# Scratch stores of the first block sent after its last word, and words placed by a model in which TensorE waits for them

## The chip, the cores and the metric

One core of one Trainium2 chip runs the kernel. The time is the device time of the whole program in microseconds; of three runs of the kernel before the median is 587.93 us (587.58 to 592.4). The engines are named as in the profile: PE is the matrix engine (TensorE, with PEld its weight loads), DVE the vector engine, ACT the scalar engine, POOL is GpSimd, and SP is the queue from which nearly all DMAs are issued.

## The reference

Three stages follow one another on 1536 tokens of width 512: attention with four sink tokens and a window of 128, a dense layer with a leaky rectifier, and a layer of eight experts with a capacity.

```python
attn_out = _attn_ref(q, k, v, n_sink=4, window=128)      # 2 x 8 heads x 768 x 64
x = attn_out.transpose(0, 2, 1, 3).reshape(1536, 512)
h = x @ w_in                                             # w_in  512 x 2048, float64
x = (np.maximum(0.01 * h, h) @ w_out).astype(float32)    # w_out 2048 x 512, float64
...                                                      # x then goes through the experts: each token to one of 8
```

The two weights of the dense layer are 64-bit floats in memory. The kernel turns them into 32-bit floats itself.

## The kernel before, in words

The tokens go through the dense layer in six blocks of 256. Attention for the tokens of the next block is cut into small steps, which are put between the matmuls of the current block. The first block (`block0`, L2080) is special, because the weights are still being loaded and converted while it runs.

**Weights.** `w_in` and `w_out` are each cut into 16 chunks, f = 0 to 15, x = 0 for `w_in` and x = 1 for `w_out`. `FFN.seq` gives the order, numbered n: (0,0), (0,1), then (1,0) to (15,0) as n = 2 to 16, then (1,1) to (15,1) as n = 17 to 31. `FFN.load` (L978) puts the 512 KB of a chunk into one of five raw buffers (`RAW = 5`). `FFN.convert` (L1002) makes three DVE instructions of a chunk, called words here: low word (L1014), sign (L1018), tail (L1024). From n = 4 on the chunks are converted in pairs (4,5), (6,7), ...: low, low, sign, sign, tail, tail. When a chunk's words have been emitted, the load of chunk n + 5 is emitted on SP; it needs the raw buffer that the tail of chunk n releases.

**Split.** For products in fp32r a converted chunk is split in two parts, wh on ACT (L1042) and wl on POOL (L1043). `w_in` chunks from f = 5 on are split before their first use, `w_out` chunks from f = 10 on as well (`AHEAD = (5, 10)`); the others are used whole in block 0 and split later. SBUF doesn't hold all the parts, so those of f = 0, 1, 14 and 15 are also stored to a scratch in HBM (L1047) and read back two blocks later (L1068). In `split` each store is emitted right after its part.

**Order of block 0.** PE first makes `hps` for f = 0 to 15 (L1090, `ffn.first`), and then adds up `y` for f = 0 to 13 (L1138, `ffn.second`); f = 14 and 15 are done in block 1. Between them lie 21 attention steps, five units' worth: per unit of a tile and a group of heads the turn (L561) and its low part on DVE (L583, L587), the scores (L614) with a masked copy and a maximum on DVE (L624, L629), the exponentials on ACT (L637), the norm (L645, L646 on DVE, L648 on POOL), the transpose (L672, copied by ACT at L684 and masked by POOL at L687), the product with v (L710) and its low part on DVE (L729, `pv_low`). The scores take four PSUM buffers in a ring of four, and the last of these is the one that `pv_low` of the unit before reads.

**What sets the order.** Every engine runs its instructions in the order in which the program emits them, SP its DMAs too: a DMA that has to wait holds back all that stand behind it. On DVE the words are placed among the attention work by a small planner, `Pace` (L63). It keeps two clocks, `pe` and `dve`. Each piece of PE work adds its cost to `pe` (L69), a word adds `WORD_US = 0.6` to `dve`, and an attention step on DVE sets `dve` to the later of both clocks plus its cost, after `fill` has placed words while `dve < pe + SLACK` (`SLACK = 1.5`). `need` (L2001) places words at once where a chunk is about to be used. PE's clock does not wait for words in the kernel before.

Of the kernel before, what the change touches and what calls it, by code (L numbers as in the profile page):

```python
# [8 lines left out]
F32 = mybir.dt.float32  # L9
# [35 lines left out]
SLACK = 1.5  # L45
AHEAD = (5, 10)
WORD_US = 0.6
ROUTE = (2, 4, 6, 9, 10, 11, 14)
HOLD, TAIL = 4, 1
QUIET = 2  # L50
# [2 lines left out]


class Call:
    def __init__(self, f, us):
        self.f, self.us = f, us

    def __call__(self):
        self.f()  # L60
# [2 lines left out]
class Pace:  # L63


    def __init__(self):
        self.pe = self.dve = 0.0
        self.fill = lambda: None

    def tensor(self, us):  # L70
        self.pe += us

    def vector(self, us, wait=0.0):
        self.fill()
# [873 lines left out]
class FFN:  # L948
# [12 lines left out]
    def __init__(self, nc, pools, A, xt, cap):  # L961
        self.nc, self.p, self.A = nc, pools, A
        self.xt, self.CAP = xt, cap
        self.DM, self.DFF = A["shape_in"]
        self.K = self.DM // P
        self.NF = self.DFF // P
        self.wide = A["w_wide"]
        self.w, self.v, self.raw, self.g, self.y = {}, {}, {}, {}, {}
        self.ahead, self.x0 = AHEAD, []
        self.seq = [(0, 0), (0, 1)] + [(f, x) for x in range(2) for f in range(1, self.NF)]  # L970
        self.phase, self.late = 0, {}
        n = max(0, self.NF - self.CAP)
        self.saved = set(range(n)) | set(range(self.NF - n, self.NF))
        self.scr = self.p["dram"].tile([self.NF, 4, P, 512], F32, name="wscr") if n else None
# [23 lines left out]
    def convert(self, n, bank):  # L998


        nc, c = self.nc, self.p["c"]
        if n >= len(self.seq):  # L1002
            return []
        f, x = self.seq[n]
        at = {}

        def low_word():
            at["w"] = self.raw[f, x].rearrange("p (n two) -> p n two", two=2)
            if bank:
                pool, tag = self.bank(n % 2)  # L1010
                at["u"] = self.p[pool].tile([P, 512], I32, tag=tag, name="word")
            else:
                at["u"] = at["v"] = c.tile([P, 512], I32, tag="c", name="cvt")
            nc.vector.tensor_scalar(at["u"], at["w"][:, :, 1], 3, 0x3FFFFFF8, op0=ALU.logical_shift_left,  # L1014
                                    op1=ALU.bitwise_and)

        def sign():
            nc.vector.scalar_tensor_tensor(at["u"], at["w"][:, :, 1], -0x40000000, at["u"], op0=ALU.bitwise_and,  # L1018
                                           op1=ALU.bitwise_or)

        def tail():
            if bank:
                at["v"] = c.tile([P, 512], I32, tag="c", name="cvt")
            nc.vector.scalar_tensor_tensor(at["v"], at["w"][:, :, 0], 29, at["u"], op0=ALU.logical_shift_right,  # L1024
                                           op1=ALU.bitwise_or)

        def take():
            r = self.raw.pop((f, x))
            if not self.wide:
                at["v"] = c.tile([P, 512], F32, tag="c", name="cvt")  # L1030
                nc.vector.tensor_copy(at["v"], r)
            self.v.setdefault(f, {})[x] = at["v"].bitcast(F32)

        return [Call(g, WORD_US) for g in (low_word, sign, tail) if self.wide] + [Call(take, 0 if self.wide else WORD_US)]

    def split(self, f, x, eng):

        nc, c = self.nc, self.p["c"]
        t = self.v[f].pop(x)
        h = c.tile([P, 512], F32R, tag="c", name="wh")  # L1040
        l = c.tile([P, 512], F32R, tag="c", name="wl")
        nc.scalar.copy(h, t)  # L1042
        eng.tensor_tensor(out=l, in0=t, in1=h.bitcast(F32), op=ALU.subtract)  # L1043
        self.w.setdefault(f, {})[x] = (h, l)
        if f in self.saved:
            for a, t in enumerate((h, l)):
                nc.sync.dma_start(out=self.scr[f, 2 * x + a], in_=t.bitcast(F32))  # L1047

    def split_x0(self):

# [812 lines left out]
def build(tc, A, n_sink, window, capacity):  # L1863
    nc = tc.nc
# [13 lines left out]
    with ExitStack() as es:  # L1878
# [32 lines left out]
        pace = Pace()  # L1911
# [15 lines left out]
        if ring:  # L1927
# [3 lines left out]
            ffn = FFN(nc, p, A, xt, FFN.CAP)  # L1931
# [13 lines left out]
        if not ring:  # L1945
            pool(rawst, "raw", bufs=nraw, side="right")
            ffn = FFN(nc, p, A, xt, FFN.CAP - FEWER // 4)
# [18 lines left out]
        def some(calls, n):  # L1966
            for f in calls[:n]:
                f()
            del calls[:n]
# [12 lines left out]
        def word():  # L1982

            if not conv:
                if chunk >= len(ffn.seq):
                    return False
                conv.extend(convert())
            f = conv.pop(0)
            f()
            pace.dve += f.us  # L1990
            return True

        def fill():

            while started and pace.dve < pace.pe + SLACK and word():
                pass
# [3 lines left out]
        def need(f, x):  # L2000

            while x not in ffn.v.get(f, ()) and x not in ffn.w.get(f, ()):
                word()
# [13 lines left out]

        rate = max(1, -(-rt.NU * rt.E // ROUTE[4]))
        ex = Experts(nc, tc, p, A, rt, ident)
# [18 lines left out]
        def second():  # L2038
            j, f, i = pending.pop(0)
            if j == 0:  # L2040
                need(f, 1)
                pace.tensor(1.4 if ffn.in_parts(0, f, 1) else 1.88)
            if j == 1:
                split(0, f, 1)
            last = i == ffn.NF - 1
            if j == late and i >= ffn.NF - HOLD:

                ffn.second(j, f, i == 0, last, range(TPB - 1))
                held.append((j, f, i))
                if last:  # L2050
                    for t in range(TPB - 1):
                        rt.evac(j * TPB + t, ffn.y[j][t])
                return
            ffn.second(j, f, i == 0, last, range(TPB))
            del ffn.g[j, f]
            if j == 0:
                splits.extend([(f, 1)] * (not ffn.in_parts(0, f, 1)))
            elif i < n_ev or j == late:
                del ffn.w[f]
            if j > 1 and i < n_ev:  # L2060
                ffn.reload(ffn.order(j)[ffn.CAP + i])
            if last:
                ts = tuple(range(j * TPB, (j + 1) * TPB))
                for t, y in zip(ts, ffn.y.pop(j)):
                    rt.evac(t, y)
                routing.extend(route(ts, True))
                if j == late - 2 and rt.NU:
                    routing.insert(-1, ex.rank)
# [11 lines left out]
        def block0():  # L2080

            NF, last_t, ndone = ffn.NF, 2 * TPB - 1, 0
            pace.pe, pace.dve = 0.0, 1.7
            count = next((n + 1 for n, x in enumerate(steps) if x[0] == last_t), len(steps))
            for s in range(2 * NF - LAG):
                x, f = divmod(s, NF)
                if x == 0:
                    need(f, 0)
                    ffn.first(0, f)
                    pace.tensor(1.42 if ffn.in_parts(0, f, 0) else 1.95)  # L2090
                    if not ffn.in_parts(0, f, 0):
                        splits.append((f, 0))
                    ffn.leak(0, f)
                    if f == 0 and ffn.ahead[0] < NF:
                        ffn.split_x0()
                    fill()
                    for a in range(f + 2 if f else 0, f + 3):
                        if ffn.ahead[0] <= a < NF:
                            need(a, 0)
                            ffn.split(a, 0, nc.gpsimd)  # L2100
                    if f == NF - 1:
                        while conv:
                            word()
                        ffn.phase = 1
                        for a in range(LAG):
                            ready(a)
                else:
                    pending.append((0, f, f))
                    second()
                    fill()  # L2110
                    if f + LAG < NF - 1:
                        ready(f + LAG)
                    if splits and not splits[0][1]:
                        split(1)
                while ndone < min(count, max(1, count * (s + 1) // (2 * NF - LAG - 1))):
                    step()
                    ndone += 1
                fill()
            while word():
                pass  # L2120
            pending.extend((0, f, f) for f in range(NF - LAG, NF))
            ffn.phase = 2

        started = 1
# [6 lines left out]
        for j in range(1, NB):  # L2131
# [9 lines left out]
            for i, f in enumerate(ffn.order(j)):  # L2141
# [20 lines left out]
                some(clears, rate)  # L2162
                if routing and i in ROUTE:
                    routing.pop(0)()
# [86 lines left out]
```

## Time and profile before

| | |
|---|---|
| median of 3 runs | 587.93 us (587.58 to 592.4) |
| the profiled execution, its own time | 592.37 us |
| its span | 590.6 us |
| mean granted clock of TensorE | 0.975 |
| PE busy / PEld / DVE / ACT / POOL | 561.6 / 482.3 / 342.4 / 292.0 / 186.1 us |
| DVE words of the pairs, L1014 + L1018 + L1024 | 28 chunks of 3 |
| scratch stores L1047 | 16 of 256 KB |

PE is busy for 95% of the span, but this is an average: block 0 ends at 105.4 us, and in it DVE is the fuller engine. The stretches are best read one by one, with the granted clock beside the busy times, since a busy PE at a lower clock gives less. The profiled execution lies 4.4 us above the median.

### The profile page before, as it was taken

How to read it: one execution, taken by the hardware profiler on the slowest of the kernel's cores; microseconds unless marked ns; L12 is line 12 of the kernel's file. 1: busy time of each engine (PE TensorE's matmuls, PEld its weight loads, DVE VectorE, ACT ScalarE, POOL GpSimd, SP SyncE). 2: the span in 40 equal slices, each digit the busy share in tenths (PEclk: the TensorE clock that was granted, in tenths of full speed). 3: DMA queues.
4: the chain of work that ended last, by engine and by line, in shares of the span. 5: the costliest groups of instructions: out<-in, count | busy, mean ns of one | idle time of the engine just before them, and what ended most of it. 6: DMA issues, size and time to landing. Idle time of an engine off the chain costs nothing.

```text
span 590.6 us, 11359 instructions
## 1 busy us (share of the span) xinstructions
PE 561.6 (95%) x3801; PEld 482.3 (82%) x3801; DVE 342.4 (58%) x823; ACT 292.0 (49%) x859; POOL 186.1 (32%) x330
## 2 busy tenths in 40 slices
PE   8988979999999999999999999999799989999993
PEld 7777636888888888888888888878699888988782
DVE  6997878667434544444435422765467656636992
ACT  6766635766444445444444333552345434425771
POOL 5665667722432243224222331231102000001110
PEclk9998989999999999999999999999699979999998
DMA  8885794699333023302320257560557645444940
GB/s 232 239 261 163 268 296 133 216 278 346 91 108 90 19 72 90 109 19 63 89 72 2 83 162 248 172 191 28 188 177 232 224 150 191 144 157 140 329 145 7
DMA packets 83577, 91.85 MB, mean 156 GB/s; under 512 B 42979, under 2 KB 51171, under 8 KB 83488
## 3 DMA queue, kind: packets, MB, share of 16 engines
q1 hardware_dynamic: 81504, 85.68, 47.6%
q0 software_dynamic: 1984, 5.13, 2.4%
q8 instruction: 38, 0.62, 0.5%
q14 instruction: 51, 0.42, 0.2%
HBM read 72.01 MB, written 20.09 MB: 156 GB/s over the span
## 4 chain that ended last, share of the span: by engine, by line
PE 71%; issue 8%; DVE 7%; DMA 7%; POOL 3%; ACT 2%; another core or an unknown queue 0%; POOLq 0%; SPq 0%; DVEq 0%; ACTq 0%
PE hps L1090 20%; PE y L1138 19%; PE ph L1585 11%; PE py L1634 8%; PE ops L710 3%; PE sps L614 2%; DMA out<-ys,gt 2%; DVE word L1018 2%; DVE word L1014 1%; POOL wl L1043 1%; DMA places<-x,rsi 1%; DMA craw<-in_moe_w 1%; DVE cvt L1024 1%; PE pps L672 1%; DMA rawo<-in_moe_w_out 1%
## 5 line engine op out<-in xcount | busy, mean ns | idle before, releaser
L1138 PE MATMUL y<-wh,gp 128*128 128x512 f32 x344 | 126.8, 409 | 1.2 <-ACT gp L1118 0.7
L1120 POOL TENSOR_TENSOR gp<-g,gp 128x256 fp32r<-128x256 f32 x77 | 57.1, 742 | 181.8 <-ACT gp L1118 167.7
L1109 DVE TENSOR_TENSOR g<-hps,g 128x256 f32<-128x256 f32 x80 | 33.7, 422 | 104.2 <-ACT g L1108 103.8
L1090 PE MATMUL hps<-xth,wh 128*128 128x256 f32 x320 | 92.0, 288 | 0.4 <-DVE g L1109 0.4
L1090 PE MATMUL hps<-xth,wl 128*128 128x256 f32 x320 | 90.6, 283 | 0.0
L1090 PE MATMUL hps<-xtl,wh 128*128 128x256 f32 x320 | 90.5, 283 | 0.0
L1449 DVE TENSOR_TENSOR cw<-craw,cw 128x512 fp32r<-128x512 f32 x128 | 83.3, 695 | 8.6 <-ACT cw L1447 6.8
L1138 PEld LDWEIGHTS y<-wh,gp 128*128 128x128 f32 x344 | 64.4, 188 | 16.2 <-ACT gp L1118 1.5
L1447 ACT CAST cw<-craw 128x512 fp32r<-128x512 f32 x112 | 63.4, 620 | 23.7 <-PE py L1634 23.1
L1108 ACT ACTIVATE g<-hps 128x256 f32<-128x256 f32 x80 | 30.6, 382 | 85.2 <-PE hps L1090 84.8
L1138 PE MATMUL y<-wl,gp 128*128 128x512 f32 x172 | 67.6, 393 | 0.6 <-POOL wl L1043 0.6
L1585 PE MATMUL ph<-xt,cw 128*128 128x256 f32 (+2 forms) x444 | 64.6, 312 | 0.0
L1634 PE MATMUL py<-cw,ht 128*128 128x512 f32 x264 | 63.9, 398 | 0.3 <-DVE ht L1622 0.3
L1090 PEld LDWEIGHTS hps<-xth,wh 128*128 128x128 f32 x320 | 60.4, 189 | 4.4 <-DVE g L1109 1.3
L1585 PEld LDWEIGHTS ph<-xt,cw 128*128 128x128 f32 x444 | 63.6, 212 | 0.1
L1090 PEld LDWEIGHTS hps<-xtl,wh 128*128 128x128 f32 x320 | 60.3, 188 | 2.2
L1090 PEld LDWEIGHTS hps<-xth,wl 128*128 128x128 f32 x320 | 60.2, 188 | 0.0
L1634 PEld LDWEIGHTS py<-cw,ht 128*128 128x128 f32 x264 | 49.0, 188 | 11.6 <-DVE ht L1622 0.7
L1643 POOL DMA_INDIRECT out<-ys,gt x11 | 11.3, 1032 | 120.1 <-DVE ys L1642 114.5
L1118 ACT CAST gp<-g 128x256 fp32r<-128x256 f32 x80 | 32.9, 411 | 21.7 <-DVE g L1109 21.7
L1138 PEld LDWEIGHTS y<-wl,gp 128*128 128x128 f32 x172 | 32.5, 189 | 5.3 <-POOL wl L1043 1.2
L637 ACT ACTIVATE pm<-pm,mx 128x132 f32<-128x132 f32 (+1 forms) x80 | 31.8, 401 | 10.1 <-DVE mx L629 10.1
(247 smaller groups left out, 996.6 us busy)
## 6 DMA issues: line engine op xcount, KB each, us to landing
craw<-in_moe_w SPq DMA_DIRECT2D x128, 256.0 KB, 3.4
rawi<-in_moe_w_in SPq DMA_DIRECT2D x16, 512.0 KB, 4.8
rawo<-in_moe_w_out SPq DMA_DIRECT2D x16, 512.0 KB, 5.9
places<-zero SPq DMA_DIRECT2D x24, 257.0 KB, 5.8
wh<-wscr SPq DMA_DIRECT2D x16, 256.0 KB, 2.9
wl<-wscr SPq DMA_DIRECT2D x16, 256.0 KB, 2.8
xg<-places SPq DMA_DIRECT2D x12, 257.0 KB, 4.3
natv<-in_v SPq DMA_DIRECT2D x12, 256.0 KB, 4.3
```

What stands on the lines that cost most here:

```text
L637: self.nc.scalar.activation(a, a, AF.Exp, bias=mx[:, pr, e:e + 1], accum_out=su[:, pr, e, 0:1])
L710: nc.tensor.matmul(ps[64 * e:64 * e + 64, pr, :], lhsT=l, rhs=r, start=(x == 0 and not (late and pr)), stop=(x == len(mm[0]) - 1 and not l ...
L1090: nc.tensor.matmul(ps, lhsT=w, rhs=x, start=(n == 0), stop=(n == len(mm) - 1))
L1108: nc.scalar.activation(g, ps, AF.Copy, scale=0.01)
L1109: nc.vector.tensor_tensor(out=g, in0=ps, in1=g, op=ALU.max)
L1118: nc.scalar.copy(gp[:, 0], g)
L1120: eng.tensor_tensor(out=gp[:, 1], in0=g, in1=gp[:, 0].bitcast(F32), op=ALU.subtract)
L1138: nc.tensor.matmul(y, lhsT=l, rhs=r, start=(start and n == 0), stop=(stop and n == len(mm) - 1))
L1447: nc.scalar.copy(h, t)
L1449: eng.tensor_tensor(out=l, in0=t, in1=h.bitcast(F32), op=ALU.subtract)
L1585: nc.tensor.matmul(self.ph[f][:, sl], lhsT=self.w[e, "a", h, k][w][:, f * P:(f + 1) * P], rhs=self.xt[:, a, k, sl], start=(m == 0), stop=( ...
L1634: nc.tensor.matmul(self.py[n], lhsT=x, rhs=w, start=(h == 0 and f == 0 and m == 0), stop=(h == self.NH - 1 and f == self.HF - 1 and m == 2))
```

## The change

Two edits. Stores: `split` no longer issues its stores but puts them in a list, and `FFN.store` issues the whole list after block 0's last word; from then on (`phase > 1`) each split stores at once, as before. Planner: when the last word of a chunk is placed, the `dve` clock is noted under the chunk's key; a PE product that uses this chunk then starts, in the model, no earlier than that time, and `PARTS_US = 2.0` later if it uses the two parts.

```diff
+PARTS_US = 2.0
...
-    def tensor(self, us):
-        self.pe += us
+        self.ready = {}
+
+    def tensor(self, us, key=None, wait=0.0):
+        self.pe = max(self.pe, self.ready.get(key, -1.0) + wait) + us
...
-        return [Call(g, WORD_US) for g in (low_word, sign, tail) if self.wide] + [Call(take, 0 if self.wide else WORD_US)]
+        return [Call(g, WORD_US) for g in (low_word, sign, tail) if self.wide] + [Call(take, 0 if self.wide else WORD_US, (f, x))]
...
         if f in self.saved:
-            for a, t in enumerate((h, l)):
-                nc.sync.dma_start(out=self.scr[f, 2 * x + a], in_=t.bitcast(F32))
+            self.stores += [(f, 2 * x + a, t) for a, t in enumerate((h, l))]
+            if self.phase > 1:
+                self.store()
+
+    def store(self):
+        while self.stores:
+            f, n, t = self.stores.pop(0)
+            self.nc.sync.dma_start(out=self.scr[f, n], in_=t.bitcast(F32))
...
             pace.dve += f.us
+            if f.key:
+                pace.ready[f.key] = pace.dve
...
-                pace.tensor(1.4 if ffn.in_parts(0, f, 1) else 1.88)
+                pace.tensor(*(1.4, (f, 1), PARTS_US) if ffn.in_parts(0, f, 1) else (1.88, (f, 1)))
...
-                    pace.tensor(1.42 if ffn.in_parts(0, f, 0) else 1.95)
+                    pace.tensor(*(1.42, (f, 0), PARTS_US) if ffn.in_parts(0, f, 0) else (1.95, (f, 0)))
...
             while word():
                 pass
             pending.extend((0, f, f) for f in range(NF - LAG, NF))
+            ffn.store()
             ffn.phase = 2
```

## Rows read from the trace of the kernel before

**Rows 1.** Stretches: busy us and counts per engine, granted clock, DMA share, GB/s.
```profile
39.50:49.00 9.50, 7.96 (x65) 7.28 (x65) 7.87 (x19) 6.12 (x21) 6.30 (x6) 1.00 0.91 259
49.00:54.00 5.00, 2.48 (x15) 2.07 (x15) 5.00 (x9) 3.80 (x12) 2.47 (x3) 0.90 0.55 178
54.00:57.00 3.00, 2.89 (x16) 2.59 (x15) 0.86 (x4) 2.62 (x10) 2.55 (x2) 0.60 0.54 146
...
66.00:79.80 13.80, 13.80 (x69) 6.98 (x67) 9.21 (x21) 9.74 (x33) 11.60 (x14) 1.00 0.87 297
79.80:83.00 3.20, 0.08 (x2) 0.09 (x1) 2.68 (x5) 0.67 (x4) 2.38 (x4) 1.00 0.70 284
83.00:87.00 4.00, 4.00 (x9) 2.16 (x10) 4.00 (x8) 0.13 (x1) 0.00 (x0) 0.58 0.77 261
...
94.40:105.44 11.04, 9.96 (x59) 6.80 (x58) 8.72 (x17) 6.69 (x22) 9.58 (x13) 1.00 0.22 50
```

**Rows 2.** Waits of PE from 105 to 540 us: in total, times, longest.
```profile
PE px L1566 <- DMA xg<-places: 2.6, 1, 2.6
```

**Rows 3.** Waits of DVE from 20 to 105.5 us.
```profile
DVE ri L645 <- ACT pm L637: 5.2, 3, 2.0
DVE word L1014 <- DMA rawo<-in_moe_w_out: 3.8, 2, 3.1
DVE pm L624 <- ACT pm L623: 2.2, 3, 1.6
DVE vh L530 <- ACT vh L528: 0.4, 1, 0.4
```

**Rows 4.** SP's issues in order: start, duration, line, DMA.
```profile
50.14 0.94 SPq L986 DMA_DIRECT2D rawo<-in_moe_w_out  x2
...
59.96 0.32 SPq L1047 DMA_DIRECT2D wscr<-wl  x1
60.37 0.88 SPq L986 DMA_DIRECT2D rawo<-in_moe_w_out  x2
...
73.48 0.44 SPq L1047 DMA_DIRECT2D wscr<-wl  x1
74.01 9.74 SPq L986 DMA_DIRECT2D rawo<-in_moe_w_out  x6
...
96.46 0.38 SPq L172 DMA_DIRECT2D natq<-in_q  x1
104.73 0.34 SPq L1047 DMA_DIRECT2D wscr<-wh  x1
```

**Rows 5.** DVE in order of time; in brackets idle time before and its releaser.
```profile
53.01 1.28 DVE L1024 SCALAR_TENSOR_TENSOR cvt<-rawi,word 128x512 int32<-128x512 int32 x2
...
66.73 1.27 DVE L1024 SCALAR_TENSOR_TENSOR cvt<-rawo,word 128x512 int32<-128x512 int32 x2
...
80.32 0.69 DVE L1014 TENSOR_SCALAR word<-rawo 128x512 int32<-128x512 int32 x1 [3.08 <-DMA rawo<-in_moe_w_out]
...
99.55 1.29 DVE L1018 SCALAR_TENSOR_TENSOR word<-rawo,word 128x512 int32<-128x512 int32 x2
100.74 1.28 DVE L1024 SCALAR_TENSOR_TENSOR cvt<-rawo,word 128x512 int32<-128x512 int32 x2
103.69 0.16 DVE L645 TENSOR_REDUCE ri<-su 128x4 f32<-128x8 f32 x1 [1.66 <-ACT pm L637]
```

**Rows 6.** Tile rawo: time from issue to landing of its 16 loads.
```profile
DMA to landing us min/median/max: 3.3/5.9/8.2
```

**Rows 7.** PE in order of time, at the scores after a `pv_low` and at y of f = 6.
```profile
61.50 0.39 PE L614 MATMUL sps<-kTh,qT 64*128 64x264 f32 x1 [0.39 <-DVE xtl L729]
82.95 3.04 PE L1138 MATMUL y<-cvt,gr 128*128 128x512 f32 x4 [3.12 <-DVE cvt L1024]
```

**Rows 8.** POOL in order of time, near the end of block 0.
```profile
88.00 1.07 POOL L648 TENSOR_TENSOR pm<-pm,ri 128x528 f32<-128x528 f32 x1 [5.81 <-DVE ri L646]
103.62 0.74 POOL L1120 TENSOR_TENSOR gp<-gr,gp 128x256 fp32r<-128x256 f32 x1
```

More of the change, by code (lines that the diff above doesn't have):

```diff
@@ L55, with __init__ @@
 class Call:
-    def __init__(self, f, us):
-        self.f, self.us = f, us
+    def __init__(self, f, us, key=None):
+        self.f, self.us, self.key = f, us, key
     def __call__(self):
@@ L970, in __init__ @@
         self.seq = [(0, 0), (0, 1)] + [(f, x) for x in range(2) for f in range(1, self.NF)]
-        self.phase, self.late = 0, {}
+        self.phase, self.late, self.stores = 0, {}, []
         n = max(0, self.NF - self.CAP)
```

## The prediction

> **What bounds the kernel now.** I first looked where PE waits. After block 0 the largest wait of PE up to 540 us is 2.6 us, for the gather of the experts' tokens [rows 2]; so from 105.4 us on the program runs at PE's own pace, and whatever block 0 ends earlier should reach the end undiminished. I therefore count only what happens before 105.4 us.
>
> Next the stretches of block 0. PE is idle 1.54 us in 39.5 to 49, 2.52 us in 49 to 54, 3.12 us in 79.8 to 83 and 1.08 us in 94.4 to 105.44, and it loses 0.40 x 3.00 = 1.2 us and 0.42 x 4.00 = 1.7 us in the two stretches in which the granted clock averages 0.60 and 0.58, that is, lies partly at 1.2 GHz [rows 1]. Together 11.2 us: the ceiling of what PE can get back here.
>
> Then DVE, which feeds PE with words. Two words take 100.74 - 99.55 = 1.19 us, so one takes 0.595 us and a chunk of three 1.79 us; the last pair is done at about 102.0 us [rows 5]. Before this DVE waits for the exponentials of an attention unit (5.2 us less the 1.66 us at 103.69, which come after the last word, leave 3.5), for raw `w_out` chunks (3.8), for the copied scores (2.2) and once for ACT (0.4) [rows 3, 5]: 9.9 us in which no word is made although words are what PE lacks.
>
> Last the SP queue. The words of chunks 14 and 15 end at 54.3 us, which frees the buffers for chunks 19 and 20; their loads go out at 60.37, right behind the store of wl of f = 14 (59.96), which had to wait for POOL. Chunks 18 and 19 are done at 68.0, but loads 23 and 24 go out at 74.01, behind the store issued at 73.48 [rows 4, 5]. Load 23 then lands so late that DVE stands 3.08 us until 80.32, and PE's y of f = 6, which needs the tail of chunk 22, stands 3.12 us and then runs four products in 3.04 us at the lower clock [rows 5, 7].
>
> **The change, part by part.** *Stores.* Ten stores (f = 14, 15, 0, 1 of `w_in`, f = 14 of `w_out`, two each) leave the loads' way and go out together. That removes the 6 us by which loads 19, 20 and 23, 24 are late. What it adds: ten issues of about 0.33 us, 3.3 us on SP [rows 4], and 2.6 MB, some 8.8 us at the 297 GB/s of the fullest stretch [rows 1]. They come behind the last raw load and the loads of q and k for tile 5; SP is free there from 96.8 to 104.73 [rows 4]. Only the last two wait for a part (POOL's wl of f = 14), and behind them stand the next stores and the clearing of the experts' places. I cost it at nothing; without that cover it would be 3.3 us on transfers that PE needs only in block 1.
>
> *Planner.* No instruction is added or taken away; PE, ACT and POOL keep their order, and only DVE's changes, with the raw loads on SP that follow the words. Working the two clocks of the model through the 30 rounds of block 0 gives the new order. The first 22 entries on DVE stay. From the norm of the unit (2,0) on, PE's clock is held back by words, so `fill` sees a later `pe` and places more words ahead of attention work: norm (2,0) and turn (2,1) come 4 words later, scores (2,1) 4, norm (2,1) and turn (3,0) 6, `pv_low` and scores (3,0) 2 and 3, norm (3,0), turn, `pv_low` and scores (3,1), norm (3,1) and turn (4,0) 8 each, `pv_low` and scores (4,0) 6 and 7; the rest stays. So the waits for exponentials and for copied scores (3.5 + 2.2 us) are filled with words. The 0.4 us stays.
>
> *New waits for raw chunks.* With five buffers, an odd chunk n + 5 is loaded once the tail of chunk n is done, and its first word follows eight words later, 8 x 0.595 = 4.76 us, plus any attention work between. The median landing is 5.9 us [rows 6]. In the new order nothing stands between for chunks 23 and 29 (1.14 us of wait each); a norm and a turn, about 0.97 us, stand between for 19 and 25 (0.17 us each); for 17, 21, 27 and 31 scores stand between as well, and nothing is left. Sum 2.6 us. By the fastest landing, 3.3 us, it is 0; by the slowest, 8.2, it is 3.44 x 2 + 2.47 x 2 + about 1.5 x 2 + 1.9 + 0.6 = 17.3 us. I take the median, since loads now go out in pairs and no longer in the bunch of six that the row of 9.74 us at 74.01 shows.
>
> *Sum on DVE.* 9.9 - 0.4 - 2.6 = 6.9 us earlier. POOL follows: its work for f = 10 to 13 starts with a norm that waits 5.81 us for DVE and ends with gp at 104.36, shortly before block 1 [rows 8]; an earlier norm shifts that chain with it.
>
> *Can PE follow?* Attention work that comes later brings PE new waits: the seventh product of a scores group already waits 0.39 us for `pv_low` [rows 7], because that frees its PSUM buffer. Following the chain with the durations of the rows, I get about 0.8, 1.5 and 1.4 us at scores (3,0), (3,1) and (4,0), and 1.7 us left of the wait around f = 11 and 12. With the 1.5 us before 45 us, which stay, that is 6.9 us of waits; the rest of PE's 11.2 us, 4.3, would be the gain if PE's visible losses were all of it. The same chain followed to the end of block 0, with the small gaps between rows counted, ends at about 97.8 us, 7.6 us earlier. I take DVE's 6.9, between the two, as DVE is the engine whose stream ends last.
>
> **Against which time.** The profiled execution took 592.37 us, 4.4 us over the median; the sum gives 585.5 us for it. I take the same 6.9 us from the median: 587.93 - 6.9 = **581.0 us**. If part of the 4.4 us was block 0's own late landing, less is to be gained; that is a rival below. A measurement of this kernel can tell about 1% from no change, here 5.9 us: faster means below 582.05, slower above 593.8.
>
> **The clock.** Two falls lie in block 0, each after PE had stood: 2.52 us in 49 to 54, 3.12 us in 79.8 to 83. The 1.54 us in 39.5 to 49, in short pieces, brought none [rows 1]. The sum counts no fall, since the waits that I expect are short pieces like those. A rule speaks against that: the Trainium skill, "TensorE: Matmul & The Clock Gate", section "A second HAM failure mode: psum-queue depth-cycling", says that a PE which often stands for a moment for its PSUM buffers swings between full and half clock. By that rule the time would be that of rival B; no row here shows a fall after short waits alone.
>
> **Rivals.**
> - *A, PE takes the wait over* (0.20). The scores wait longer for `pv_low` than I have it and each attention unit ends later. For it: up to eight words, 4.76 us, now stand before work that PE waits for. Against: at most places DVE lags PE by less. The gain is PE's 4.3 us less one more such wait of 1.3: 3 us, 584.9 us.
> - *B, the clock falls after the new waits* (0.08). Two more stretches like those in the rows, 1.2 and 1.7 us: 6.9 - 2.9 = 4.0, 583.9 us.
> - *C, it does little* (0.09). The late landing belongs to slow executions like the profiled one; in the others the stores cost nothing and words only change places: 0 to 2 us, 587 us.
> - *D, slower* (0.08). Raw loads land as late as in the worst row. The place is DVE's queue in the second half of block 0: a word that waits for its load now has up to eight words' worth of attention work behind it. Price by the sum above: 17.3 + 0.4 - 9.9 = 7.8 us slower, 595.7 us. It decides from a landing of about 7.1 us on. For it: the DMAs carry 284 to 297 GB/s at 66 to 83 us [rows 1]. Against: 2 MB of stores leave that stretch.
> - *E, more* (0.05). Loads land in 4.76 us or less, so DVE gains 9.9 - 0.4 = 9.5 us: 578.4 us. PE's ceiling less its first 1.54 us, 9.7 us, allows it; but then none of its new waits may be real.
>
> The forecast has 0.50, with a range of its own of 578.4 to 583.6 (gain 9.5 to 4.3); some 0.42 of it lies below 582.05. The range to hold 8 of 10 goes from 577.5 to 587.0: it takes in A, B, nearly all of E and most of C. Faster: 0.42 + 0.05 of E + 0.03 from A and B = 0.50. Slower: 0.07 of D. Same: the remaining 0.43.
>
> **What would show it.** Right: SP's raw loads follow each tail at once, with no store between them before the last one; DVE's waits for exponentials and for copied scores are near 0 up to its last word, which ends near 95 us; y of f = 6 starts without a wait and at full clock; block 1's first hps starts near 98.5 instead of 105.44. Wrong: new waits of DVE for rawo above 3 us (D), or of PE for `pv_low` and for the exponentials above 5 us (A), or granted clocks below 1 around 75 or 87 us (B). If all steps show and the time does not follow, the cover after block 0 was not PE's own pace.

## The result, and the profile after

The changed kernel takes 581.87 us (median of six runs, 578.09 to 583.52), the kernel before 587.87 us on the same chip (six runs, 587.12 to 592.4): a ratio of 0.9886 with a 95% interval of 0.9839 to 0.9932. On a second chip the ratio was 0.9867 (0.9815 to 0.992). So it is faster, by a little over 1%, as forecast; the forecast was 581.0 us.

The mark by which I compare is the first product of block 1, PE's first `hps<-xth,wh`: 105.4 us before, 97.1 us after, 8.3 us earlier instead of the 6.9 us forecast. The same stretch in both kernels, from 39.5 us to that mark, is shown here, first before and then after; the columns are those of [rows 1], and the stretches left out of the second list also have a granted clock of 1.00:

```profile
39.50:105.44 65.94, 57.17 (x352) 39.41 (x353) 53.11 (x110) 38.46 (x127) 43.40 (x50) 0.95 0.67 213
```

```profile
49.00:54.00 5.00, 3.67 (x27) 3.02 (x26) 5.00 (x10) 5.00 (x19) 4.15 (x5) 1.00 0.77 248
54.00:57.00 3.00, 3.00 (x37) 2.70 (x37) 2.96 (x8) 1.86 (x6) 1.46 (x2) 1.00 0.75 236
...
79.80:83.00 3.20, 3.20 (x29) 1.96 (x29) 3.17 (x9) 0.65 (x2) 0.73 (x2) 1.00 1.08 351
83.00:87.00 4.00, 4.00 (x24) 2.02 (x21) 3.85 (x9) 2.99 (x10) 3.94 (x6) 1.00 0.05 17
87.00:97.11 10.11, 9.90 (x61) 6.91 (x59) 5.64 (x14) 7.04 (x23) 10.11 (x13) 1.00 0.46 139
39.50:97.11 57.61, 53.96 (x353) 37.49 (x353) 52.06 (x110) 38.11 (x127) 43.50 (x50) 1.00 0.73 226
```

The counts agree within one record on every engine: the same work in 57.61 instead of 65.94 us. PE's idle time falls from 65.94 - 57.17 = 8.77 to 3.65 us, 5.1 us of the gain. Its busy time falls by 57.17 - 53.96 = 3.2 us, because the granted clock is now 1.00 in every stretch and no longer 0.60 and 0.58 in two of them [rows 1]; 0.05 x 65.94 = 3.3 us says the same. So the gain is waits and the clock falls that followed them.

DVE's waits from 20 to 105.5 us after, for [rows 3], and three of its instructions in order of time, for [rows 5]:

```profile
DVE ri L647 <- ACT pm L639: 3.8, 1, 3.8
...
DVE word L1016 <- DMA rawo<-in_moe_w_out: 0.6, 1, 0.6
```

```profile
72.06 0.69 DVE L1016 TENSOR_SCALAR word<-rawo 128x512 int32<-128x512 int32 x1 [0.62 <-DMA rawo<-in_moe_w_out]
...
90.30 1.28 DVE L1026 SCALAR_TENSOR_TENSOR cvt<-rawo,word 128x512 int32<-128x512 int32 x2
95.34 0.16 DVE L647 TENSOR_REDUCE ri<-su 128x4 f32<-128x8 f32 x1 [3.76 <-ACT pm L639]
```

The last pair of words ends near 91.6 us (102.0 before). Of the two waits only the 0.62 us at 72.06 lie ahead of it; the 3.8 us for the exponentials are at 95.34, when no word is left. Between these two rows of the first view stand three for ACT, 3.1 us in all, that come behind the last word as well. SP's queue after, for [rows 4]:

```profile
46.91 6.79 SPq L988 DMA_DIRECT2D rawo<-in_moe_w_out  x4
...
65.75 11.62 SPq L988 DMA_DIRECT2D rawo<-in_moe_w_out  x6
...
92.65 0.58 SPq L1055 DMA_DIRECT2D wscr<-wh  x1
...
98.89 0.60 SPq L1055 DMA_DIRECT2D wscr<-wl  x1
```

No store stands between the raw loads; the ten come together, 92.65 to 99.5 us. PE's waits from 39 to 106 us after, and its rows at the places of [rows 7]:

```profile
PE hps L1098 <- POOL wl L1045: 2.8, 4, 0.9
PE sps L616 <- DVE xtl L731: 0.4, 1, 0.4
PE y L1146 <- POOL gp L1128: 0.2, 1, 0.2
```

```profile
73.13 0.39 PE L616 MATMUL sps<-kTh,qT 64*128 64x264 f32 x1 [0.43 <-DVE xtl L731]
...
76.06 3.60 PE L1146 MATMUL y<-cvt,gr 128*128 128x512 f32 x8
...
96.06 0.74 PE L1146 MATMUL y<-wh,gp 128*128 128x512 f32 x2 [0.18 <-POOL gp L1128]
```

At 76.06 stands y of f = 6 (with the four products of f = 7): no wait, 0.45 us a product, where before it stood 3.12 us and then took 0.76 us for each.

**Behind the mark.** The two profiled executions differ by 592.37 - 579.82 = 12.55 us, 4.2 more than the mark. Most of the rest is in the experts, before and after:

```profile
474.59 0.63 PE L1566 MATMUL ph<-ident,xg 128*128 128x128 f32 x4 [1.56 <-DVE ys L1642]
474.98 16.03 PE L1585 MATMUL ph<-xt,cw 128*128 128x128 f32 x108
```

```profile
465.32 0.63 PE L1574 MATMUL ph<-ident,xg 128*128 128x128 f32 x4 [1.01 <-DVE ys L1650]
465.70 12.89 PE L1593 MATMUL ph<-xt,cw 128*128 128x128 f32 x108
```

The same 108 products take 3.1 us longer before, at a granted clock of 0.79 in 475 to 491 us against 1.00 in 466 to 479 us after, and the wait ahead of them is 0.55 us longer. Nothing shows that this comes from the change: the same fall shows in some profiles of kernels with one edit or both and is absent in others (last section).

The runs speak for it too. Many of them lie on levels, each with its mean granted clock: 11 of the 74 runs of before near 591.6 us at 0.976 and 24 near 588.5 at 0.982; 4 of the 12 of after near 583.2 at 0.981 and 7 near 579.9 at 0.987. The other runs of before lie between these clocks or above them. Block 0's falls alone take 3.3 / 590 = 0.006 off the mean clock, so the level of before at 0.976 should answer to that of after at 0.981, and 0.982 to 0.987: 8.4 and 8.6 us, the mark's gain. This pairing is argued from the clocks; no profile of before on its second level was taken. The medians of all runs that have a clock beside them, but for six of before in the slow state (592.0 to 593.6 us), are 588.6 (74) and 580.5 (12), which gives 8.1; the two sets of six above give 6.0, because three of the six of after lie on the lower clock.

Only the shortest runs are closer: 583.8 at 0.994 (9 runs of before) to 578.1 at 0.992 (1 of after), 5.7 us. A mean clock of 0.994 leaves some 0.006 x 590 = 3.5 us for all falls of the program together, and block 0's alone take 3.3; so in these nine runs block 0's falls may be missing, which is not shown. The one profile at 0.994, the second of experiment 8, differs from the changed kernel's behind the mark: the experts' first group of 108 products takes 13.9 us there and 16.5 in the changed kernel, by a shorter fall.

### The profile page after: what moved, and what is told of

The parts are those of the page before. It is cut to its first block, busy times and chain, and to the rows that moved or that the text cites. A ratio compares the mean times of both kernels' runs of the same rounds, so it can differ in the third digit from the quotient of the medians.

```text
span 578.1 us, 11347 instructions
## 1 busy us (share of the span) xinstructions
PE 555.7 (96%) x3801; PEld 477.4 (83%) x3801; DVE 341.0 (59%) x823; ACT 291.5 (50%) x859; POOL 185.9 (32%) x330
## 4 chain that ended last, share of the span: by engine, by line
PE 71%; DVE 8%; issue 8%; DMA 7%; POOL 2%; ACT 2%; another core or an unknown queue 0%; POOLq 0%; SPq 0%; ACTq 0%; DVEq 0%
PE hps L1098 20%; PE y L1146 19%; PE ph L1593 10%; PE py L1642 8%; PE ops L712 3%; DMA out<-ys,gt 2%; PE sps L616 2%; DVE word L1016 2%; DVE word L1020 2%; DMA craw<-in_moe_w 1%; DMA places<-x,rsi 1%; PE pps L674 1%; PE qps L563 1%; DMA rawo<-in_moe_w_out 1%; DVE cvt L1026 1%
## 5 line engine op out<-in xcount | busy, mean ns | idle before, releaser
L1593 PE MATMUL ph<-xt,cw 128*128 128x256 f32 (+2 forms) x444 | 61.1, 301 | 0.0
L1593 PEld LDWEIGHTS ph<-xt,cw 128*128 128x128 f32 x444 | 60.0, 201 | 0.1
```

Of the source, the lines that this page charges most:

```text
L1593: nc.tensor.matmul(self.ph[f][:, sl], lhsT=self.w[e, "a", h, k][w][:, f * P:(f + 1) * P], rhs=self.xt[:, a, k, sl], start=(m == 0), stop=( ...
```

## The experiments

All kernels start from the changed one unless said otherwise. Their mark is the main reading, as it excludes the experts' levels; the ratio to the kernel before on the same chip stands beside it. A mark comes from one profile. Four kernels were profiled twice, and their marks differ by 0.02 us (before), 0.06 (changed), 0.4 (experiment 8) and 1.3 (experiment 2). By time most of these kernels can't be told apart: the ratios of experiments 2 and 4 are, in one set of runs each, about as low as that of the changed kernel.

**1. The stores alone.** The planner's clock is the old one, the stores are still kept back.

```diff
-        self.pe = max(self.pe, self.ready.get(key, -1.0) + wait) + us
+        self.pe += us
```

> The stores are held back as in the change, the planner's PE clock is that of before, so DVE's order is that of before. The mark is the start of block 1's first hps product (105.44 us before, 97.11 after). Theory S (each edit removes its own share): the raw loads go out right behind the tails, DVE's 3.8 us of waits for rawo shrink to about 1, PE's 3.12 us before y of f = 6 and the half-clock stretch behind it go; the waits for exponentials (3.5 us before the last word) stay. Mark at 100.5 to 102.5. Theory P (the planner does it all, the stores only seemed to be in the way): mark at 104.5 to 105.5. Theory J (the two need each other: free loads are of no use while DVE waits for attention): mark at 103.5 to 105.

Mark 102.4 us, 3.0 us earlier than before; ratio 0.997 (0.9935 to 1.0005). DVE's waits in 20 to 105.5 us:

```profile
DVE ri L647 <- ACT pm L639: 5.8, 3, 2.2
DVE pm L626 <- ACT pm L625: 2.0, 3, 1.6
```

The wait for raw chunks is gone (3.8 us before), those for exponentials and copied scores stand as before. So is PE's wait before y of f = 6 with the clock fall behind it (1.00 from 57 us on); the first fall is still there (0.87 in 49 to 54 us, 0.65 in 54 to 57). The late landing belonged to the stores, and gives about 3 us, as expected of theory S.

**2. The planner alone.** The stores go out at once, as before.

```diff
-            if self.phase > 1:
-                self.store()
+            self.store()
```

> The planner of the change, but each store is issued right behind its split, as before. Theory S: DVE's waits for exponentials and copied scores go, its waits for rawo stay or grow to 4 to 6 us, since the words are now asked for earlier than the loads behind the stores can land. Mark at 100 to 102.5, and with the stores-only kernel the two gains add up to the 8.3 us of the change within 1.5 us. Theory P: mark at 97 to 98.5. Theory J: the waits only move from exponentials to rawo, so that DVE's sum of waits before its last word stays above 8 us: mark at 103.5 to 105.5.

Mark 102.1 us, 3.4 us earlier; ratio 0.9888 (0.9838 to 0.9937), from six runs, more than the mark can give. It was therefore run once more on another chip:

> The planner-only kernel again. Its first profiled execution was the second slowest of six (589.4 us), with the mark at 102.1, DVE waiting 0.97 and 2.11 us for rawo and PE 3.0 us for pv_low at scores (3,1). If these waits belong to the order of loads and stores: mark at 101.5 to 102.7 again. If they belong to that execution: mark at 99 to 101, and the planner alone is worth more than the stores alone.

Mark 103.4 us, 2.0 us earlier and 0.7 behind the expected 101.5 to 102.7; ratio 0.9962 (0.9924 to 1.0001), which goes with it. SP's queue of the second run, one DVE and one PE wait, and the stretch in which they lie:

```profile
65.96 0.33 SPq L1054 DMA_DIRECT2D wscr<-wh  x1
67.32 0.33 SPq L1054 DMA_DIRECT2D wscr<-wl  x1
...
70.17 1.17 SPq L988 DMA_DIRECT2D rawo<-in_moe_w_out  x2
71.43 0.38 SPq L1054 DMA_DIRECT2D wscr<-wh  x1
71.91 0.38 SPq L1054 DMA_DIRECT2D wscr<-wl  x1
72.38 9.41 SPq L988 DMA_DIRECT2D rawo<-in_moe_w_out  x4
```

```profile
DVE word L1016 <- DMA rawo<-in_moe_w_out: 4.6, 2, 3.5
```

```profile
PE sps L616 <- DVE xtl L731: 4.5, 1, 4.5
```

```profile
66.00:79.80 13.80, 9.26 (x49) 4.92 (x48) 8.91 (x21) 4.61 (x15) 8.93 (x10) 0.86 0.93 297
79.80:83.00 3.20, 3.20 (x9) 1.76 (x8) 3.20 (x6) 1.02 (x5) 0.65 (x1) 0.55 0.31 99
```

The words are placed ahead of the attention work, but the loads that they need still stand behind the stores. DVE waits 4.6 us for them, with `pv_low` queued behind; PE's scores stand 4.5 us for that, and the clock falls to 0.55. The first fall of before, in 49 to 57 us, is gone (1.00). That is rival D's mechanism and rival A's wait in one place, and still 2 us better than before. Alone the edits give 3.0 and 2.0 to 3.4 us, together 8.3: some 2 to 3 us come only when both are made, where theory S expected 1.5 at most.

**3. Place or bytes.** As 1, but each store is emitted four `w_out` loads after its split: the bytes go back among the loads, but each store's part is long ready.

```diff
+LATER = 4
...
+            self.sent = n
+            self.store(n)
...
-        while self.stores:
-            f, n, t = self.stores.pop(0)
+        while self.stores and self.stores[0][3] + LATER <= sent:
+            f, n, t, _ = self.stores.pop(0)
```

> As the stores-only kernel, with the planner of before, but each store goes out four w_out loads later than its split instead of after the last word: its bytes stay in the same stretch of block 0, and by then its part is done, so it holds nothing up. If the place in SP's queue was the harm: mark within 0.7 us of the stores-only kernel. If the 2 MB in the stretch were the harm (loads landing late): DVE's waits for rawo above 3 us, y of f = 6 waits again, mark at 104 or later.

Mark 102.3 us, ratio 0.9928 (0.9896 to 0.9961), no wait for raw chunks: as expected if the place does the harm. SP's queue:

```profile
68.36 0.35 SPq L1058 DMA_DIRECT2D wscr<-wh  x1
68.81 0.37 SPq L1058 DMA_DIRECT2D wscr<-wl  x1
73.97 1.72 SPq L989 DMA_DIRECT2D rawo<-in_moe_w_out  x2
```

A store that doesn't wait holds the queue for about 0.4 us. Here the eight stores of `w_in` go out between 61 and 78 us, among the loads. What they cost before was the place in the queue of a DMA whose data weren't there yet, not their 2 MB.

**4. and 5. How the words are placed.** Experiment 4 keeps the old clock of PE and lets every placement run further ahead; 5 keeps the change's clock without the extra time for the parts.

```diff
-SLACK = 1.5
+SLACK = 4.0
...
-        self.pe = max(self.pe, self.ready.get(key, -1.0) + wait) + us
+        self.pe += us
```

> The stores held back, the planner of before, but SLACK 4.0 instead of 1.5: the words are put ahead by a constant and not where PE waits. In the model's order attention work then stands 4 to 5 words later than before up to scores (2,1), by 2 and 0 at the units (2,1) and (3,0), and by 2 to 4 later on, where the change has 8. If it matters only that words come ahead of attention by some amount: mark within 1 us of 97.11. If the amount at each place matters as the sum on DVE has it: the waits for exponentials at the norms (2.0 and 1.5 us) are filled only in part, mark at 98 to 100.

```diff
-PARTS_US = 2.0
+PARTS_US = 0.0
```

> The change with PARTS_US = 0: in the model PE still waits for its words, but not 2.0 us longer for the two parts. In the model's order attention work then stands 0 words later up to the turn (2,1), 1 at scores (2,1), 2, 2, 0 and 0 up to scores (3,0), 4 at the unit (3,0)'s norm to the turn (4,0), and 2 to 3 at the end; the change has 4, 4, 6, 2, 3, 8 and 6 to 7. Theory S, in which the words that stand ahead fill DVE's waits place by place: the wait for copied scores at (2,1) (1.6 us) and most of the wait for exponentials at the norm (2,1) (2.0 us) stay, the later ones go; mark at 99 to 101.5. Rival: only that PE waits at all matters, or the later places: mark at 97 to 98.

Marks 99.2 and 100.4 us; ratios 0.9866 (0.9815 to 0.9918, four runs) and 0.9952 (0.9914 to 0.999). Both marks lie where they were expected if the amount at each place matters. Waits of DVE and of PE in 4:

```profile
DVE pm L626 <- ACT pm L625: 3.1, 2, 1.6
```

```profile
PE y L1146 <- DVE cvt L1026: 2.0, 1, 2.0
```

Experiment 5 has the same PE wait of 2.0 us and 3.8 us for copied scores. It also has PE waits that the changed kernel lacks, and the first clock fall of before is back:

```profile
PE hps L1098 <- ACT wh L1044: 1.2, 2, 1.1
```

```profile
49.00:54.00 5.00, 3.07 (x18) 2.83 (x18) 5.00 (x9) 4.55 (x15) 3.01 (x4) 0.85 0.69 230
54.00:57.00 3.00, 2.63 (x19) 2.21 (x19) 2.28 (x7) 1.98 (x8) 1.98 (x2) 0.68 1.08 358
```

A plain slack of 4 gets 3.2 of the 5.3 us that separate 1 from the changed kernel (102.4 - 99.2 of 102.4 - 97.1), the change's clock without `PARTS_US` 2.0 of them. With the stores kept back, more than half of the planner's part is thus to be had by running further ahead everywhere; the rest came with placing words by the product that needs them. Whether a still larger slack would bring it too was not run. The extra time for the parts alone is worth 100.4 - 97.1 = 3.3 us. DVE's waits for copied scores, 3.8 us without it and none with it, and the clock fall, by 0.15 x 5 + 0.32 x 3 = 1.7 us, go with it; the two overlap, and what each is worth alone is not shown.

**6. Rival D's condition.** One raw buffer fewer, so that the loads come one word group later.

```diff
-RAW = 5
+RAW = 4
```

> The change with four raw buffers instead of five, to price the term of late landing (my rival D). Each chunk's load now has 4.2 us of words (7 x 0.595) before its own first word, plus the attention work between. If a load lands in about 6 us, as the one for which the changed kernel waits (0.6 us) did: about 1.8 us per chunk that has no attention work between, some 8 to 14 us in all from chunk 14 on, mark at 103 to 110. If the loads land in 4.7 us or less as the others of the changed kernel allow: 0 to 4 us in all, mark at 97 to 101.

Mark 101.0 us, 3.9 us behind the changed kernel and 4.4 ahead of before; ratio 0.994. DVE and PE:

```profile
DVE word L1016 <- DMA rawo<-in_moe_w_out: 2.6, 3, 1.2
```

```profile
PE sps L616 <- DVE xtl L731: 1.8, 1, 1.8
```

DVE waits only 2.6 us for `w_out` (and 0.9 for `w_in`) even with loads a chunk later. The mark, at the upper end of the expected 97 to 101, lies with landings near 4.7 us, not with 6. By that, rival D, which decides from 7.1 us on, is far away. The opposite case, six buffers, was not run.

**7. Cheaper words.** Low words written to SBUF in place of PSUM, to see what still depends on DVE.

```diff
-                return ffn.convert(n, ring and started) + [Call(lambda: ffn.load(n + nraw), 0)]
+                return ffn.convert(n, False) + [Call(lambda: ffn.load(n + nraw), 0)]
```

> The change, with the first two words of a chunk written to SBUF instead of a PSUM bank (convert is called without a bank). It asks whether DVE's stream still bounds block 0. The low words that went to SBUF before block 0 took 0.41 us (396 to 469 ns) against 0.69 to PSUM, so 28 chunks save up to 28 x 0.2 = 5.6 us on DVE. If DVE is the bound and nothing else changes: mark at 92 to 94. If the sign and tail words, which then read two operands from SBUF, are slowed as the one of 1.41 us at 18 us was, or POOL's splits are (1.28 us now): mark at 97 or later, with POOL's mean per split above 1.35 us.

Mark 118.6 us, ratio 1.0248 (1.0173 to 1.0324): much slower. Signs (L1020), tails (L1026, only here) and POOL's splits (L1045), in nanoseconds as least/median/most, first in the changed kernel, then here:

```profile
L1020 DVE SCALAR_TENSOR_TENSOR word<-rawo,word x15: 683/686/693, 54.3 to 89.7; 128x512 int32<-128x512 int32 x15
...
L1045 POOL TENSOR_TENSOR wl<-cvt,wh x22: 1267/1284/1302, 34.6 to 100.9; 128x512 fp32r<-128x512 f32 x22
```

```profile
L1020 DVE SCALAR_TENSOR_TENSOR cvt<-rawo,cvt x16: 680/1198/1770, 18.0 to 109.7; 128x512 int32<-128x512 int32 x16
L1026 DVE SCALAR_TENSOR_TENSOR cvt<-rawo,cvt x16: 677/698/1776, 20.7 to 112.6; 128x512 int32<-128x512 int32 x16
...
L1045 POOL TENSOR_TENSOR wl<-cvt,wh x22: 1267/1404/1738, 37.0 to 122.4; 128x512 fp32r<-128x512 f32 x22
```

With both inputs in SBUF a sign takes up to 1.77 us instead of 0.69, and POOL's split up to 1.74 instead of 1.30. DVE hardly waits, its words are slower, and PE waits for it (the granted clock averages 0.86 up to the mark). So the question the kernel was made for stays unanswered; it says what the words in PSUM are good for. The Trainium skill, "SBUF — State Buffer", section "Who interferes with whom", says that a DVE instruction with two SBUF inputs contends with a GpSimd instruction that reads SBUF. These rows agree.

**8. What ends block 0 now.** From 87 us, ahead of the last word, to the mark POOL is busy all 10.11 us. Two of its splits, f = 12 and 13 of `w_out`, go to DVE, which has nothing left.

```diff
-                    ffn.split(f, 1, nc.gpsimd)
+                    ffn.split(f, 1, nc.vector if f in (12, 13) else nc.gpsimd)
```

> The change, with the splits of w_out chunks 12 and 13 on DVE instead of POOL. After its last word (91.6 us) DVE stands 3.8 us while POOL is busy without a gap from 84 to 98 us. If POOL's chain, not DVE, sets the end of block 0 now: POOL is 2.5 us lighter, gp of f = 13 comes earlier, mark at 95 to 96.3. If PE's own products set it (9.90 of 10.11 us busy from 87 on): mark at 96.5 to 97.2. Later than 97.5 if DVE is held up by the splits, which wait for ACT.

> The kernel with the splits of w_out chunks 12 and 13 on DVE again, beside the changed kernel on one chip. Mark at 96.2 within 0.3 us, 0.9 earlier than the changed kernel's; by this the median should be about 1 us (0.2%) lower, which lies below what the scatter of single runs (578 to 584 us for the changed kernel) lets one see with certainty.

> The changed kernel again, on the chip of the next run, to see how much of its time is block 0 and how much is the rest. Expected: mark (block 1's first hps product) at 97.1 within 0.3 us. From the mark to the end of the span either 480 to 482.5 us, when the experts' third group of 108 products runs at full clock (12.6 us), or 485 to 486, when it runs partly at half clock (15.7 us).

Marks 96.2 and, on another chip, 96.6 us (0.1 above what was expected), beside 97.2 of the changed kernel on that chip; ratios 0.9815 (0.9741 to 0.9889) and 0.9845 (0.9793 to 0.9897), beside 0.9867 of the changed kernel. POOL in order of time, first run:

```profile
90.71 0.81 POOL L1128 TENSOR_TENSOR gp<-gr,gp 128x256 fp32r<-128x256 f32 x1 [0.52 <-ACT gp L1126]
...
94.40 0.73 POOL L1128 TENSOR_TENSOR gp<-gr,gp 128x256 fp32r<-128x256 f32 x1 [0.52 <-ACT gp L1126]
```

POOL now waits, and PE is busy for 13.20 of the 13.20 us from 83 to 96.2. So POOL's chain did set the end of the changed kernel, but it was worth 0.6 to 0.9 us: PE stands next. Behind the mark the changed kernel took 481.2 us on that chip, with the experts' third group at full clock. By time, ten runs give a median of 579.6 us against 580.5 for twelve of the changed kernel, which is beneath what these runs can tell apart.

**9. The stall before.** The kernel before, profiled once more on another chip.

> The kernel before, profiled once more. My rival C said that its late landing (3.08 us of DVE at 80.3 us) belongs to slow executions. If it does: mark below 103.5 in an execution near the median. If the wait belongs to the order on SP: mark at 105.4 within 0.7 us, DVE's wait for rawo at chunk 23 again, and the scatter of the total lies behind the mark.

Mark 105.4 us again, in an execution of 592.0 us.

```profile
DVE word L1014 <- DMA rawo<-in_moe_w_out: 2.8, 1, 2.8
```

```profile
PE y L1138 <- DVE cvt L1024: 2.8, 1, 2.8
```

The wait of y of f = 6 is there once more (3.1 us in the first profile). This execution too is one of the longest. No profile of a short run of before was taken, and whether the stall is as long in those stays open. Rival C's size, 0 to 2 us, is refuted by the times: even between the shortest runs lie 5.7 us.

## Why the prediction was right, and where its sizes were off

- **The forecast and the median.** That 581.87 us lies 0.9 us from the forecast is in part luck. The mark moved by 8.3 us, 1.4 more than the sum, and half of the first six runs of after lie on the lower clock; on the second chip the median of six runs is 580.0 us.
- **The waits on DVE.** Right in kind: 9.9 us of waits ahead of the last word became 0.6 us, and the raw loads follow their tails. The 0.4 us for `vh`, which were to stay, went as well. Experiments 1 and 2 show which edit removes which: the raw waits go with the stores, those for exponentials and scores with the planner.
- **The new waits for raw chunks.** This is the mis-sized term: 2.6 us forecast from the median landing of the kernel before, 0.62 us measured, at one place. The trace of after lists no landing times, but two rows of DVE bound one. The wait forecast for chunk 23 (1.14 us) did not come:

```profile
61.45 1.28 DVE L1026 SCALAR_TENSOR_TENSOR cvt<-rawo,word 128x512 int32<-128x512 int32 x2
...
66.23 1.28 DVE L1016 TENSOR_SCALAR word<-rawo 128x512 int32<-128x512 int32 x2
```

The first tail, of chunk 18, ends near 62.1 us and frees the buffer; the second low word, of chunk 23, starts near 66.8 without a wait. So this load landed within 4.7 us, while that of chunk 25, issued from 65.75, took till 72.06, some 6.3 us. Experiment 6 speaks for landings nearer to 4.7 than to 6 us too. The row of 9.74 us at 74.01 [rows 4], which I read as a bunch of six loads, is three pairs in one row: its last pair could go only once the tails of chunks 22 and 23 had ended, at 83.4 us. By the measured 0.62 the sum would have been 9.9 - 0.4 - 0.6 = 8.9 us, against 8.3 at the mark.
- **DVE as the engine that ends last.** This step failed, without harm to the number. DVE's last word came 10.4 us earlier (91.6 instead of the forecast 95), but the mark only 8.3: POOL and PE take over, and between the last word and the mark lie 5.5 us instead of 3.4. Experiment 8 shows POOL's part of it, 0.6 to 0.9 us.
- **PE's new waits.** Far too large: 0.8 + 1.5 + 1.4 us forecast for `pv_low`, 0.43 measured, and none at f = 11 and 12. PE's own estimate of 4.3 us was too small mainly by that; measured, 5.1 us of idle time and 3.2 us of clock came back. Its ceiling of 11.2 us was 0.9 short as well, since it left out the small losses in the other stretches (8.77 + 3.3 = 12.1). Where DVE does wait for loads, as in the planner alone, `pv_low` is late and PE stands 4.5 us: rival A's mechanism exists, and the stores' move took away its cause. The chain followed to the end of block 0, 7.6 us, was the nearest of the three estimates; it alone held all engines, and I should have taken it.
- **The clock.** Right: none of the short waits, up to 0.9 us, lowered it, and the two falls of before, 2.9 us, came back with the waits that preceded them (3.2 us measured). The Trainium skill's rule ("TensorE: Matmul & The Clock Gate", section "A second HAM failure mode: psum-queue depth-cycling") that many short stops make it swing does not show in the changed kernel: 3.65 us of stops in 57.61 us, and 1.00 in every stretch. Experiment 5 comes nearer to it, though its waits there are for the parts from ACT and POOL. Its PE stood 1.08 and 0.85 us between 48 and 52 us, and the clock fell behind that; in experiment 4 one stop of 2.0 us brought no fall. So that short pieces bring no fall held for the changed kernel and is not shown beyond it.
- **The stores at the end.** Nothing shows that they cost anything. Ten issues took 92.65 to 99.5 us, 6.8 us instead of 3.3, beside the end of block 0; from the mark to 540 us the longest wait of PE's for a transfer is still that for the experts' tokens (2.7 us, 2.6 before; [rows 2]).
- **Nothing but PE's pace behind 105 us.** Right for the waits, but the time there is not constant: 481.0 us from the mark to the end of the span after, 485.2 before, for the most part by the experts' clock.

## What to carry to other kernels

In a queue that runs in order, a store that waits for its producer costs what stands behind it; move it behind the last urgent load, or late enough that its data are ready. When one edit brings loads earlier and another uses them earlier, try both together, for each alone may only move the wait. When runs lie on levels that differ by a third of the gain, read it at a mark inside the program.

## What the runs showed of the hardware that was not expected

- The fall in the experts' third group costs 3.1 us in one execution and is absent in the next. In 14 profiles it stands in four, 15.98 to 16.09 us for the 108 products (both of the kernel before, the first of experiment 2, and 6), and the group takes 12.9 us in the other ten. Before it PE stood for `ys` 1.29, 1.56, 1.61 and 1.62 us in the four; in nine of the others 1.00 to 1.10 us, in one (experiment 5) 1.57 us. So the fall goes with the longer wait, but the wait alone doesn't decide it.
- Issuing one store took 0.43 to 1.19 us on SP where ten follow one another, 0.32 us where they stand alone [rows 4].
- A tail word of DVE, which only gains a second SBUF input at the same shape, has a median of 0.70 us instead of 0.68 but takes up to 1.78 instead of 0.69 while POOL works; a sign, whose output moves from PSUM to SBUF as well, has a median of 1.20 us instead of 0.69 (experiment 7).
- The length of one stop of PE doesn't decide whether the granted clock falls behind it: one of 2.0 us brought no fall (experiment 4), two of 1.08 and 0.85 us close together did (experiment 5).
